# Score tiles of ten query rows by one transfer each, and a ring of eight tiles begun five steps ahead

## The chip, the cores and the metric

The kernel runs on one core of one Trainium2 chip. The metric is the device time of one execution in microseconds (us). A second value stands beside it in the profile: the span, from the first to the last instruction of the profiled execution.

## The reference

Attention whose heads are mixed before and after the softmax, then two MLP-mixer blocks. Only the attention is touched by the change:

```python
# q, k, v: (2, 12, 448, 64); w_pre, w_post: (12, 12)
scores = scale * np.matmul(q, k.transpose(0, 1, 3, 2))
scores = np.einsum('bhij,hg->bgij', scores, w_pre)
scores = scores - np.max(scores, axis=-1, keepdims=True)
attn = np.exp(scores)
attn = attn / (np.sum(attn, axis=-1, keepdims=True) + 1e-09)
attn = np.einsum('bhij,hg->bgij', attn, w_post)
return np.matmul(attn, v).astype(np.float32)
```

Behind it stand a token-mixing and a channel-mixing MLP (`_moe_ref`) and a gated MLP (`_moe2_ref`). They take about the last 320 us of the span.

## The kernel before

**Chunks.** Each of the two batches is cut into four chunks of 120, 120, 120 and 88 query rows. For a chunk, `qk` multiplies q by k for all twelve heads (six head pairs, six calls) and copies the result into a score tile S in SBUF: one query row to a partition, its 12 x 448 scores behind each other. S has two halves, partitions 0 to 63 and 64 to 127, and half of the chunk's rows stand in each. There are two buffers for S, so chunk x+2 overwrites chunk x.

**Steps.** The head mix contracts over heads, so heads must lie in partitions. `b_dma` therefore copies rows of S into tiles P with (query row, head) in the partitions: five query rows give 60 partitions. A step handles 20 query rows: two tiles P (r = 0, 1), each with two transfers of five rows (h = 0, 1) that land in partitions 0 to 59 and 64 to 123. A transfer's five source rows lie `nb` partitions apart: 12 in a chunk of 120, 8 in the chunk of 88. There are 23 steps to a batch, 46 in all; the last step of each chunk of 88 is half a step.

**What a step does.** `b_pre` (TensorE) multiplies the tiles P by a block-diagonal `wp`; `b_exp` takes the row maximum (VectorE) and the exponential (ScalarE); `b_norm` scales the post-mix weights (VectorE, GpSimd); `b_post` mixes heads after the softmax and turns the result (TensorE); `b_turn` copies it out of PSUM (VectorE). When a chunk's steps are done, `av` multiplies by v (TensorE), and VectorE and ScalarE copy its result.

**Order.** The order is written out by hand. Iteration i of the main loop issues `b_pre(i + LP)`, then `qk` for a later chunk, `b_exp(i + LP)`, `b_norm(i + 1)`, `b_post(i)`, `b_turn(i)`, `av` where a new chunk starts, and `b_dma(i + LD)`, with LD = 4 and LP = 2. So the transfers of a step stand two iterations ahead of the `b_pre` that reads them. The tiles P come from a pool of `NP_BUFS` = 2 (LD - LP + 1) = 6. The six `qk` calls of a chunk are spread over the iterations up to LD ahead of its first step, leaving out the iterations that have an `av`.

**Queues.** Every transfer of this stage but two is issued by SyncE (SP), in program order: the P transfers and the loads of q, k, v and, at the end of the stage, of weights. Each DMA also waits until the one issued eight before it has landed (eight semaphores in turn).

Of the kernel before, what the change touches and what calls it, by code (L numbers as in the profile page):

```python
# [8 lines left out]
F32 = mybir.dt.float32  # L9
# [7 lines left out]
AX = mybir.AxisListType  # L17
PSUM = bass.MemoryType.PSUM

LD, LP = 4, 2  # L20
NP_BUFS = 2 * (LD - LP + 1)

WB, RB, SQ = 3, 3, 5
# [7 lines left out]
def tile_kernel(ctx, tc, q, k, v, w_pre, w_post, w_tok1, w_tok2, w_ch1, w_ch2,  # L31
                w_u, w_v, g_ln, w_sg, b_sg, w_out, out):
    nc = tc.nc
    B, D, H, S = 2, 64, 12, 448
    P = 128
# [10 lines left out]
    IB = 10  # L46
    CH = [(0, 120), (120, 120), (240, 120), (360, 88)]
# [8 lines left out]
    xT = xpool.tile([P, NCC, T], F32, name="xT")  # L56
# [3 lines left out]
    wp = const.tile([P, 64], F32, name="wp")  # L60
# [167 lines left out]
    for n, w in enumerate(chw):  # L228
        p_ch.append(piece(w, P, NCC, P))
        if n in V_EARLY:  # L230
            j = V_EARLY[n]
# [3 lines left out]
    for o in GATE_ORDER.split():  # L235
        j = int(o[1])
# [40 lines left out]
    ap_ = actx.enter_context(tc.tile_pool(name="attn", bufs=1))  # L277
# [11 lines left out]
    vn, qn, KX, SS = {}, {}, {}, {}  # L289
# [32 lines left out]
    steps = []  # L322
# [8 lines left out]
    st = [dict() for _ in range(NB)]  # L331
    HB = IB // 2
    HW = HB * H
    NK = S // 64

    def b_dma(i):

        b, c, p, ne = steps[i]
        nb = CH[c][1] // IB
        ss = SS[b, c].rearrange("(a p) f -> a p f", a=2)  # L340
        st[i]["P"] = []
        for r in range(2):
            t = ap_.tile([P, S], F32, tag="P", name=f"P{i}_{r}", bufs=NP_BUFS)
            if ne == 2:
                j = 2 * p + r
                for h in range(2):
                    nc.sync.dma_start(out=t[64 * h:64 * h + HW],
                                      in_=SS[b, c][64 * h + j:64 * h + j + (HB - 1) * nb + 1:nb])
            else:
                m = CH[c][1] % (2 * IB) // 2  # L350
                r0 = 64 * r + HB * nb
                nc.sync.dma_start(out=t[:m * H], in_=SS[b, c][r0:r0 + m])
            st[i]["P"].append(t)

    def b_pre(i):
        b, c, p, ne = steps[i]
        rows = HW if ne == 2 else CH[c][1] % (2 * IB) // 2 * H
        ps = st[i]["pre"] = pair(psB, "B", f"pre{i}")
        for r, cols in enumerate(HALVES):
            for e in range(ne):  # L360
                rs = slice(64 * e, 64 * e + rows)
                nc.tensor.matmul(ps[cols, e, :S], lhsT=wp[rs], rhs=st[i]["P"][r][rs], start=True, stop=True)  # L362
        st[i]["P"] = None

    def b_exp(i):
        ne = steps[i][3]
# [10 lines left out]
    def b_norm(i):  # L377
# [6 lines left out]
        for e in range(ne):  # L384
            wt = ap_.tile([P, 64], F32, tag="wt", name=f"wt{i}_{e}", bufs=6)
            nc.gpsimd.tensor_scalar(wt[:, :HW], wd["post"], rr[:, e:e + 1], 1.0, op0=ALU.mult, op1=ALU.mult)  # L386
            st[i]["w"].append(wt)
# [4 lines left out]
    def b_post(i):  # L392
# [5 lines left out]
        for e in range(ne):  # L398
            E, wt = st[i]["e"][e], st[i]["w"][e]
            for s in range((NK + 1) // 2):  # L400
                for x, cols in enumerate(HALVES):
                    t = min(2 * s + x, NK - 1)
                    w = slice(0, HW) if 2 * s + 1 < NK else slice(x * HW // 2, (x + 1) * HW // 2)
                    o = e * 256 + s * HW
                    for r in range(2):
                        rs = slice(64 * r, 64 * r + HW)
                        nc.tensor.matmul(ps[cols, r, o:o + w.stop - w.start], lhsT=E[rs, t * 64:(t + 1) * 64],  # L407
# [10 lines left out]
    def av(b, c):  # L418
        s0, n = CH[c]
        nb = n // IB  # L420
        rest = n - nb * IB
        cols = IB * (nb + (rest > 0))
        ps = pair(psA, "A", f"av{b}_{c}")
        at = AT[b, c]
        for hp in range(NP):
            x, o = hp % 2, hp // 2 * cols
            for s in range(NK // 2):
                for j, out_rows in enumerate(HALVES):
                    w = vn[b, hp // 2][:, ((x * 2 + j) * (NK // 2) + s) * D:][:, :D]
                    nc.tensor.matmul(ps[out_rows, x, o:o + cols], lhsT=w,  # L430
                                     rhs=at[:, s * H + x * (H // 2) + hp // 2 * 2 + j, :cols],
                                     start=(s == 0 and hp < 2), stop=False, skip_group_check=True)
        for hp in range(NP):
            x, o = hp % 2, hp // 2 * cols
            for j, out_rows in enumerate(HALVES):
                nc.tensor.matmul(ps[out_rows, x, o:o + cols], lhsT=vn[b, hp // 2][HALVES[x], (12 + j) * D:(13 + j) * D],
                                 rhs=at[HALVES[x], NK // 2 * H + hp // 2 * 2 + j, :cols],
                                 start=False, stop=True, skip_group_check=True)
        s0 += b * S
        for x, copy in enumerate((nc.vector.tensor_copy, nc.scalar.copy)):  # L440
            src = ps[:, x, :NP // 2 * cols].rearrange("p (c k) -> p c k", k=cols)
            copy(xT[:, x::2, s0:s0 + nb * IB].rearrange("p c (i j) -> p c j i", j=nb),  # L442
                 src[:, :, :nb * IB].rearrange("p c (j i) -> p c j i", i=IB))
            if rest:
                h = rest // 2
                copy(xT[:, x::2, s0 + nb * IB:s0 + n].rearrange("p c (r i) -> p c r i", i=h),
                     src[:, :, nb * IB:].rearrange("p c (r i) -> p c r i", i=HB)[:, :, :, :h])

    CW = C // 2
# [35 lines left out]
    def turn_over(n):  # L485
        for _ in range(n):
            nc.tensor.matmul(idle[:, 0, :P], lhsT=ident, rhs=ident, start=True, stop=True)

    turn_over(8)
    scale_pre()  # L490
    both = ((psA, "A"), (psB, "B"), (psB, "B"))
    copies = (nc.scalar.copy, nc.vector.tensor_copy)
    for x in range(2):
        for i in range(NP):
            n = x * NP + i
# [29 lines left out]
    for i in range(-LD, NB):  # L525
# [35 lines left out]
        if i + LP >= NB:  # L561
            for _ in range(2):
                ps = pair(psB, "B", f"xps0_{len(turns)}")
# [95 lines left out]
    with ExitStack() as rctx:  # L659
# [5 lines left out]
        for f in range(NF):  # L665
            need(p_c1[f])
            w = parts(p_c1[f])
            for b in range(B):
                finish(*[U[cc, b] for cc in range(NCC)])
                ps = bank(f"c1ps{b}_{f}")  # L670
# [6 lines left out]
        for cc in range(NCC):  # L677
            pss = [bank(f"c2ps{b}_{cc}") for b in range(B)]
            for hf, pi in enumerate(p_c2[cc]):
                need(pi)  # L680
                w = parts(pi)
# [154 lines left out]
    for cc, b in [(0, 0), (1, 0), (0, 1), (1, 1)] + [(cc, b) for cc in range(2, NCC) for b in range(B)]:  # L836
# [3 lines left out]
        ps = bank(f"ops{b}_{cc}")  # L840
# [11 lines left out]
def layouts(q, k, v, w_pre, w_post, moe_w_tok1, moe_w_tok2, moe_w_ch1, moe_w_ch2,  # L852
            moe2_w_in, moe2_g_ln, moe2_w_sg, moe2_b_sg, moe2_w_out):

    import numpy as np

    def bits(a):

        return a.view(np.uint64) if a.dtype == np.float64 else a

    def rows(a, p):

        return bits(a).reshape(-1, p, a.shape[1]).transpose(1, 0, 2)

    def cols(a, p):

        return bits(a).reshape(a.shape[0] // p, p, -1, p).transpose(1, 2, 0, 3)

    def diagonal(w):
        h = w.shape[0]  # L870
        t = np.zeros((2, 64, 5, h), w.dtype)
        for i in range(5):
            t[:, i * h:(i + 1) * h, i] = w
        return t

    def halves(a):

        n = a.shape[-1] // 2
        nb = a.shape[-1] // 10
        rest = n - 5 * nb  # L880
        t = np.zeros((*a.shape[:-1], 2, 64), a.dtype)
        for h in range(2):
            t[..., h, :5 * nb] = a[..., h * 5 * nb:(h + 1) * 5 * nb]
            t[..., h, 5 * nb:n] = a[..., 10 * nb + h * rest:10 * nb + (h + 1) * rest]
        return t

    def tokens(w):

        t = np.concatenate([w.T, w.T])
        return t.reshape(-1, 128, t.shape[1]).transpose(1, 0, 2)  # L890

    B, H, S, D = q.shape
    qt = q.reshape(B, H // 2, 2, S, D).transpose(0, 2, 4, 1, 3).reshape(B, 2 * D, H // 2, S)
    qt = np.stack([halves(qt[..., s:s + 120]) for s in range(0, S, 120)], 2)
    whole = S // 128 * 128
    vs = v.reshape(B, H // 4, 2, 2, S, D)
    vt = vs[..., :whole, :].reshape(B, H // 4, 4, S // 128, 128, D).transpose(0, 4, 1, 2, 3, 5)
    vr = vs[..., whole:, :].transpose(0, 2, 4, 1, 3, 5).reshape(B, 128, H // 4, 2 * D)
    vt = np.concatenate([vt.reshape(B, 128, H // 4, -1), vr], -1)
    wp = diagonal(w_pre).reshape(128, 60)  # L900
    wq = diagonal(w_post).reshape(2, 64, 5, H // 4, 2, 2).transpose(0, 1, 4, 3, 5, 2).reshape(128, 60)
    half = moe2_w_in.shape[1] // 2
    arrays = {
        'q': qt,
        'k': k.reshape(B, H // 2, 2, S, D).transpose(0, 2, 4, 1, 3).reshape(B, 2 * D, H // 2, S),
        'v': vt,
        'w_pre': np.concatenate([wp, np.zeros((128, 4), wp.dtype)], 1),
        'w_post': wq,
        'w_tok1': rows(moe_w_tok1, S // 4),
        'w_tok2': rows(moe_w_tok2, 128),  # L910
        'w_ch1': cols(moe_w_ch1, 128),
        'w_ch2': cols(moe_w_ch2, 128),
        'w_u': cols(np.ascontiguousarray(moe2_w_in[:, :half]), 128),
        'w_v': rows(np.ascontiguousarray(moe2_w_in[:, half:]), 128),
        'g_ln': moe2_g_ln.reshape(-1, 128).T,
        'w_sg': tokens(moe2_w_sg),
        'b_sg': moe2_b_sg.reshape(1, S),
        'w_out': cols(moe2_w_out, 128),
    }
    return {n: np.ascontiguousarray(a) for n, a in arrays.items()}  # L920
# [34 lines left out]
```

## Time and profile before

| | us |
|---|---|
| median of 3 runs (lowest, highest) | 588.27 (586.41, 589.18) |
| the profiled execution | 587.66 |
| its span | 585.9 |
| the attention stage, in the span | about 13 to 266 |
| TensorE busy over the span | 549.0 |
| SyncE: issue of a P transfer, median | 0.737 |
| mean granted TensorE clock | 0.959 |

The profiled execution's time is 1.8 us above its span and 0.6 us below the median of the runs. TensorE (PE) is busy for 94% of the span, but a matmul that sits in the pipe counts as busy, so the chain of waits says more than the busy share. Lines of kernel.py are written L362 and so on; PEld is TensorE's weight load, SPq and the like are the engines' issue queues.

### The profile page before, as it was taken

The page shows a single profiled execution, that of the slowest core. Times are in us where ns is not written, and L with a number is a line of the kernel's source. Part 1 is how long each engine was busy: PE and PEld are TensorE (multiplying, and loading weights), DVE is VectorE, ACT ScalarE, POOL GpSimd, SP SyncE. Part 2 cuts the span into 40 slices and gives each one's busy share as a digit, 9 for nine tenths or more (in the row PEclk, how much of TensorE's full clock was granted, in tenths as well). Part 3 has the DMA queues.
Part 4 walks back from the last instruction along what each step waited for, and adds up shares of the span by engine and source line. Part 5 has one row for each costly group of instructions (what it writes and reads, how often), then busy time and mean ns, then how long its engine had stood idle before and what let it go on. Part 6 is the DMA issues. An engine that isn't in the chain of part 4 may idle for free.

```text
span 585.9 us, 14093 instructions
## 1 busy us (share of the span) xinstructions
PE 549.0 (94%) x5998; PEld 425.2 (73%) x5998; DVE 353.1 (60%) x537; ACT 239.3 (41%) x453; POOL 154.4 (26%) x185
## 2 busy tenths in 40 slices
PE   7999998889899989579999999999999999999997
PEld 4344655555455545358999999999999999888986
DVE  3354555344546543635835576777888786588882
ACT  3243545343535444634533334343333335455320
POOL 0010111011111111200492223234454454246600
PEclk9799999799989979759999999999999999999999
DMA  4365342323631315410312243434253332300332
GB/s 152 138 190 179 120 137 76 112 65 132 187 128 72 126 61 163 149 54 1 115 48 66 89 152 106 146 110 143 92 160 111 94 136 64 119 17 10 118 112 94
DMA packets 25647, 63.63 MB, mean 109 GB/s; under 512 B 2832, under 2 KB 18704, under 8 KB 25584
## 3 DMA queue, kind: packets, MB, share of 16 engines
q1 hardware_dynamic: 25296, 62.33, 32.8%
q8 instruction: 47, 0.77, 0.6%
q10 hardware_dynamic: 288, 0.39, 0.2%
q14 instruction: 16, 0.13, 0.1%
HBM read 40.70 MB, written 2.75 MB: 74 GB/s over the span
## 4 chain that ended last, share of the span: by engine, by line
PE 77%; DMA 13%; DVE 3%; ACT 3%; issue 2%; SPq 1%; POOLq 0%; POOL 0%; DVEq 0%; ACTq 0%
DMA P<-S 11%; PE pre L362 9%; PE av L430 5%; PE post L407 5%; PE c1ps L581 5%; PE c2ps L580 5%; PE c2ps L581 5%; PE c1ps L579 5%; PE c1ps L580 5%; PE c2ps L579 5%; PE qk L317 3%; PE ups L579 2%; PE ups L580 2%; PE ups L581 2%; PE vps L580 2%
## 5 line engine op out<-in xcount | busy, mean ns | idle before, releaser
L362 PE MATMUL pre<-P,wp 60*64 60x448 f32 x360 | 107.8, 587 | 12.2 <-DMA P<-S 11.4
L369 DVE TENSOR_REDUCE nm<-pre 128x2 f32<-128x896 f32 (+1 forms) x46 | 49.0, 1066 | 70.9 <-PE pre L362 70.7
L386 POOL TENSOR_SCALAR wt<-wd_post,rr 128x60 f32<-128x60 f32 x90 | 28.4, 329 | 215.5 <-DVE rr L382 174.0
L147 POOL TENSOR_TENSOR wl<-cv,wh 128x768 fp32r<-128x768 f32 x28 | 52.5, 1876 | 119.8 <-ACT wh L146 85.6
L407 PEld LDWEIGHTS post<-wt,E 60*64 60x64 f32 x2880 | 65.3, 145 | 23.0 <-issue 16.9
L374 ACT ACTIVATE E<-pre,nm 128x448 f32<-128x448 f32 x90 | 56.4, 634 | 44.4 <-DVE rc L380 34.7
L362 PEld LDWEIGHTS pre<-P,wp 60*64 60x64 f32 x360 | 24.9, 139 | 64.5 <-DMA P<-S 55.4
L407 PE MATMUL post<-wt,E 60*64 60x60 f32 (+1 forms) x2880 | 66.3, 230 | 3.8 <-ACT AT L415 2.9
L317 PE MATMUL qk<-kn,qn 64*64 64x448 f32 x384 | 58.6, 567 | 8.3 <-ACT xT L442 4.8
L319 ACT COPY S<-qk 128x896 f32<-128x896 f32 x42 | 38.1, 906 | 63.0 <-PE qk L317 59.6
L124 DVE SCALAR_TENSOR_TENSOR cv<-raw,cv 128x768 uint32<-128x768 uint32 (+3 forms) x44 | 53.2, 1209 | 1.3
L581 PE MATMUL c2ps<-r1h,wl 128*128 128x448 f32 x144 | 52.6, 365 | 0.0
L581 PE MATMUL c1ps<-uh,wl 128*128 128x448 f32 x144 | 52.6, 365 | 0.0
L580 PE MATMUL c2ps<-r1l,wh 128*128 128x448 f32 x144 | 52.6, 365 | 0.0
L579 PE MATMUL c1ps<-uh,wh 128*128 128x448 f32 x144 | 52.6, 365 | 0.0
L580 PE MATMUL c1ps<-ul,wh 128*128 128x448 f32 x144 | 52.6, 365 | 0.0
L579 PE MATMUL c2ps<-r1h,wh 128*128 128x448 f32 x144 | 52.6, 365 | 0.0
L415 DVE COPY AT<-post 128x840 f32<-128x840 f32 (+1 forms) x38 | 39.9, 1050 | 14.6 <-PE post L407 14.2
L102 ACT ACTIVATE cv<-raw 128x768 f32<-128x768 f32 (+3 forms) x44 | 36.1, 821 | 23.8 <-POOL wl L147 16.7
L126 DVE SCALAR_TENSOR_TENSOR cv<-raw,cv 128x768 uint32<-128x768 uint32 (+3 forms) x44 | 40.2, 914 | 1.1
L317 PEld LDWEIGHTS qk<-kn,qn 64*64 64x64 f32 x384 | 16.4, 135 | 30.2 <-issue 10.7
L120 DVE TENSOR_SCALAR cv<-cv 128x768 f32<-128x768 f32 (+3 forms) x44 | 30.2, 686 | 10.3 <-ACT cv L102 10.1
(187 smaller groups left out, 993.2 us busy)
## 6 DMA issues: line engine op xcount, KB each, us to landing
P<-S SPq DMA_DIRECT2D x176, 105.0 KB
raw<-in_w_ch_dram SPq DMA_DIRECT2D x24, 768.0 KB
raw<-in_w_v_dram SPq DMA_DIRECT2D x6, 512.0 KB
raw<-in_w_u_dram SPq DMA_DIRECT2D x4, 768.0 KB
raw<-in_w_out_dram SPq DMA_DIRECT2D x6, 512.0 KB
qn<-in_q_dram SPq DMA_DIRECT2D x14, 192.0 KB
vn<-in_v_dram SPq DMA_DIRECT2D x6, 448.0 KB
out_dram<-xT SPq DMA_DIRECT2D x12, 224.0 KB
```

The lines of the kernel that those rows point to most:

```text
L124: nc.vector.scalar_tensor_tensor(fi, lo, 29, fi, op0=ALU.logical_shift_right, op1=ALU.bitwise_or)
L126: nc.vector.scalar_tensor_tensor(fi, hi, 0xC0000000, fi, op0=ALU.bitwise_and, op1=ALU.bitwise_or)
L147: nc.gpsimd.tensor_tensor(dst[1], f, f32(dst[0]), op=ALU.subtract)
L317: nc.tensor.matmul(ps[cols, j, :S], lhsT=qn[b, c, i // QG][rows, i % QG, h], rhs=KX[b, i][rows], start=True, stop=True)
L362: nc.tensor.matmul(ps[cols, e, :S], lhsT=wp[rs], rhs=st[i]["P"][r][rs], start=True, stop=True)
L369: nc.vector.tensor_reduce(out=nm[:, :ne], in_=ps[:, :ne, :S], axis=AX.X, op=ALU.max, negate=True)
L374: nc.scalar.activation(t, ps[:, e, :S], AF.Exp, bias=nm[:, e:e + 1], scale=1.0, accum_out=sm[:, e:e + 1])
L407: nc.tensor.matmul(ps[cols, r, o:o + w.stop - w.start], lhsT=E[rs, t * 64:(t + 1) * 64], rhs=wt[rs, w], start=True, stop=True)
L415: copy(dst.rearrange("p g (a i) -> p a g i", i=HB), src.rearrange("p a (g i) -> p a g i", i=HB))
L579: nc.tensor.matmul(ps, lhsT=lh, rhs=rh, start=(start and i == 0), stop=False)
L580: nc.tensor.matmul(ps, lhsT=lh, rhs=rl, start=False, stop=False)
L581: nc.tensor.matmul(ps, lhsT=ll, rhs=rh, start=False, stop=(stop and i == n - 1))
```

## The change

`b_dma` makes one transfer for each tile: ten source rows, `nb` partitions apart, into partitions 4 to 123. Now `nb` is the number of steps of the chunk, so the ten rows lie 6 partitions apart in a chunk of 120 and 4 in the chunk of 88; they all lie in one half of S (tile r reads half r). A step has two transfers of 120 partitions where it had four of 60. The half step reads five rows where it read four. The tiles are eight fixed buffers `ring`, whose partitions 0 to 3 are set to zero once; `b_pre` reads partitions 0 to 63 and 64 to 123. LD is 5, so a step's transfers stand three iterations ahead of their `b_pre`, and the `qk` calls end one iteration earlier. The layouts of q, `w_pre` and `w_post` that the host prepares follow the new order of rows.

```diff
-LD, LP = 4, 2
+LD, LP = 5, 2
 NP_BUFS = 2 * (LD - LP + 1)
...
+    PAD = 64 - HW
     NK = S // 64
 
+    ring = [ap_.tile([P, S], F32, name=f"P{n}") for n in range(NP_BUFS)]
+
     def b_dma(i):
 
         b, c, p, ne = steps[i]
-        nb = CH[c][1] // IB
-        ss = SS[b, c].rearrange("(a p) f -> a p f", a=2)
-        st[i]["P"] = []
+        nb = CH[c][1] // (2 * IB)
         for r in range(2):
-            t = ap_.tile([P, S], F32, tag="P", name=f"P{i}_{r}", bufs=NP_BUFS)
-            if ne == 2:
-                j = 2 * p + r
-                for h in range(2):
-                    nc.sync.dma_start(out=t[64 * h:64 * h + HW],
-                                      in_=SS[b, c][64 * h + j:64 * h + j + (HB - 1) * nb + 1:nb])
-            else:
-                m = CH[c][1] % (2 * IB) // 2
-                r0 = 64 * r + HB * nb
-                nc.sync.dma_start(out=t[:m * H], in_=SS[b, c][r0:r0 + m])
-            st[i]["P"].append(t)
+            j = 64 * r + p
+            src = SS[b, c][j:j + (IB - 1) * nb + 1:nb] if ne == 2 else SS[b, c][64 * r + IB * nb:64 * r + IB * nb + HB]
+            nc.sync.dma_start(out=ring[(2 * i + r) % NP_BUFS][PAD:PAD + ne * HW], in_=src)
 
     def b_pre(i):
...
-                rs = slice(64 * e, 64 * e + rows)
-                nc.tensor.matmul(ps[cols, e, :S], lhsT=wp[rs], rhs=st[i]["P"][r][rs], start=True, stop=True)
-        st[i]["P"] = None
+                rs = slice(64 * e, 64 * e + 64 - PAD * e)
+                nc.tensor.matmul(ps[cols, e, :S], lhsT=wp[rs], rhs=ring[(2 * i + r) % NP_BUFS][rs], start=True, stop=True)
...
+    for t in ring:
+        nc.gpsimd.memset(t[:PAD], 0.0)
     turn_over(8)
```

SyncE's queue at the end of batch 0's chunk 2 and the start of its chunk 3. P16 and P17 below are the tiles of chunk 2's last steps, S0_3 is the score tile of chunk 3, qn1 the q of batch 1. Before:

```order
L347 DMA P16_0_1226<-S0_2_451 60x1x448 x2
L347 DMA P16_1_1229<-S0_2_451 60x1x448 x2
L347 DMA P17_0_1292<-S0_2_451 60x1x448 x2
L347 DMA P17_1_1295<-S0_2_451 60x1x448 x2
L347 DMA P18_0_1358<-S0_3_912 60x1x448 x2
L347 DMA P18_1_1361<-S0_3_912 60x1x448 x2
L299 DMA qn1_1_0_1364<-in_q_dram 128x384
```

The same place now (tiles are named by their place in the ring):

```order
L346 DMA P0_94<-S0_2_383 120x1x448
L346 DMA P1_95<-S0_2_383 120x1x448
L73 DMA gl_70<-in_g_ln_dram 128x4
L346 DMA P2_96<-S0_2_383 120x1x448
L346 DMA P3_97<-S0_2_383 120x1x448
L346 DMA P4_98<-S0_3_822 120x1x448
L346 DMA P5_99<-S0_3_822 120x1x448
L299 DMA qn1_1_0_1250<-in_q_dram 128x384
```

Two issues stand where four stood, and the load of q behind them stays where it was.

TensorE's queue from the `av` of chunk 0 on, up to the first `pre` of step 10 (qk0_2_4 and qk0_2_5 are the last two `qk` calls of chunk 2). Before:

```order
L436 MATMUL av0_0_714<-AT0_0_277,vn0_2_442 64x120 x4
L362 MATMUL pre9_773<-P9_0_651,wp_69 64x448 x2
L362 MATMUL pre9_773<-P9_1_654,wp_69 64x448 x2
L317 MATMUL qk0_2_4_778<-kn0_2_102,qn0_2_1_255 64x448 x4
L407 MATMUL post7_799<-wt7_0_675,E7_0_605 64x60 x12
L407 MATMUL post7_799<-wt7_0_675,E7_0_605 64x30 x4
L407 MATMUL post7_799<-wt7_1_677,E7_1_607 64x60 x12
L407 MATMUL post7_799<-wt7_1_677,E7_1_607 64x30 x4
L362 MATMUL pre10_839<-P10_0_765,wp_69 64x448 x2
L362 MATMUL pre10_839<-P10_1_768,wp_69 64x448 x2
L317 MATMUL qk0_2_5_844<-kn0_3_104,qn0_2_1_255 64x448 x4
```

The same place now:

```order
L427 MATMUL av0_0_698<-AT0_0_279,vn0_2_447 64x120 x4
L354 MATMUL pre9_753<-P2_96,wp_69 64x448 x2
L354 MATMUL pre9_753<-P3_97,wp_69 64x448 x2
L317 MATMUL qk0_2_5_758<-kn0_3_112,qn0_2_1_257 64x448 x4
L398 MATMUL post7_779<-wt7_0_659,E7_0_593 64x60 x12
L398 MATMUL post7_779<-wt7_0_659,E7_0_593 64x30 x4
L398 MATMUL post7_779<-wt7_1_661,E7_1_595 64x60 x12
L398 MATMUL post7_779<-wt7_1_661,E7_1_595 64x30 x4
L354 MATMUL pre10_817<-P4_98,wp_69 64x448 x2
L354 MATMUL pre10_817<-P5_99,wp_69 64x448 x2
L317 MATMUL qk0_3_0_823<-kn0_0_102,qn0_3_0_376 64x448 x4
```

The last `qk` of chunk 2 now stands right behind the `av`, one iteration earlier than before, and the next chunk's first `qk` has taken its old place; the number of matmuls is the same.

## Rows read from the trace of the kernel before

**Rows 1.** The page: chain shares by line; two groups (busy, mean ns); P transfers

```profile
DMA P<-S 11%; PE pre L362 9%; PE av L430 5%; PE post L407 5%; PE c1ps L581 5%; PE c2ps L580 5%; PE c2ps L581 5%; PE c1ps L579 5%; PE c1ps L580 5%; PE c2ps L579 5%; PE qk L317 3%; PE ups L579 2%; PE ups L580 2%; PE ups L581 2%; PE vps L580 2%
...
L369 DVE TENSOR_REDUCE nm<-pre 128x2 f32<-128x896 f32 (+1 forms) x46 | 49.0, 1066 | 70.9 <-PE pre L362 70.7
...
L415 DVE COPY AT<-post 128x840 f32<-128x840 f32 (+1 forms) x38 | 39.9, 1050 | 14.6 <-PE post L407 14.2
...
P<-S SPq DMA_DIRECT2D x176, 105.0 KB
```

**Rows 2.** Windows between ends of av: length, engines' busy time (count), clock, DMA share, GB/s

```profile
15.00:62.90 47.90, 45.26 (x668) 22.29 (x664) 21.07 (x34) 16.37 (x42) 4.78 (x16) 0.93 0.53 168
62.90:90.70 27.80, 26.23 (x580) 15.54 (x576) 14.95 (x26) 13.65 (x31) 4.01 (x14) 1.00 0.36 123
90.70:122.10 31.40, 28.38 (x588) 17.02 (x584) 14.82 (x25) 14.45 (x32) 3.61 (x12) 0.89 0.27 86
122.10:145.80 23.70, 21.90 (x464) 12.50 (x460) 11.50 (x21) 11.00 (x24) 2.70 (x9) 1.00 0.31 106
145.80:176.40 30.60, 27.61 (x580) 16.05 (x576) 14.76 (x26) 13.48 (x32) 3.59 (x12) 0.94 0.48 157
176.40:202.80 26.40, 25.20 (x581) 15.18 (x576) 14.84 (x26) 13.65 (x31) 3.59 (x12) 1.00 0.26 96
202.80:233.70 30.90, 26.76 (x548) 15.76 (x544) 12.12 (x24) 14.49 (x32) 3.58 (x12) 0.89 0.36 113
233.70:265.60 31.90, 20.93 (x356) 16.07 (x348) 15.23 (x32) 13.48 (x26) 4.07 (x6) 0.63 0.31 95
```

**Rows 3.** The chain of waits from 92 us: start, length, what

```profile
92.39 0.98 PE qk L317 x8
93.37 0.90 PE post L407 x64
94.28 0.78 PE pre L362 x8
95.06 0.75 PE qk L317 x8
...
99.24 5.37 DMA P<-S
```

**Rows 4.** The chain of waits at an av, from 117 us

```profile
117.44 3.84 PE av L430 x72
121.28 0.82 PE av L436 x24
...
122.12 0.80 DVE xT L442
...
122.94 0.79 ACT xT L442
```

**Rows 5.** The chain of waits in the first steps

```profile
15.75 3.25 DMA P<-S
...
46.02 7.78 DMA P<-S
```

**Rows 6.** SyncE's issues by line: ns, shortest/median/longest; first and last start

```profile
L347 SPq DMA_DIRECT2D P<-S x176: 720/737/1729, 13.2 to 227.2; - x176
L352 SPq DMA_DIRECT2D P<-S x4: 647/666/1340, 116.1 to 230.9; - x4
...
L299 SPq DMA_DIRECT2D qn<-in_q_dram x14: 334/488/1246, 2.8 to 159.5; - x14
```

**Rows 7.** Timeline of SyncE: start, length, issues

```profile
13.20 9.46 SPq L347 DMA_DIRECT2D P<-S  x12
```

**Rows 8.** Windows in which P transfers run back to back (columns as in Rows 2)

```profile
84.50:92.50 8.00, 7.04 (x174) 5.81 (x170) 4.01 (x6) 2.12 (x5) 0.60 (x2) 1.00 0.34 124
...
211.00:213.00 2.00, 0.58 (x16) 0.27 (x9) 0.17 (x1) 2.00 (x5) 0.60 (x2) 1.00 0.30 97
215.00:219.00 4.00, 4.00 (x58) 2.37 (x61) 0.87 (x1) 0.00 (x0) 0.00 (x0) 0.50 0.27 88
```

More of the change, by code (lines that the diff above doesn't have):

```diff
@@ L333, in tile_kernel @@
     HW = HB * H
+    PAD = 64 - HW
     NK = S // 64
+    ring = [ap_.tile([P, S], F32, name=f"P{n}") for n in range(NP_BUFS)]
     def b_dma(i):
         b, c, p, ne = steps[i]
-        nb = CH[c][1] // IB
-        ss = SS[b, c].rearrange("(a p) f -> a p f", a=2)
-        st[i]["P"] = []
+        nb = CH[c][1] // (2 * IB)
         for r in range(2):
-            t = ap_.tile([P, S], F32, tag="P", name=f"P{i}_{r}", bufs=NP_BUFS)
-            if ne == 2:
-                j = 2 * p + r
-                for h in range(2):
-                    nc.sync.dma_start(out=t[64 * h:64 * h + HW],
-                                      in_=SS[b, c][64 * h + j:64 * h + j + (HB - 1) * nb + 1:nb])
-            else:
-                m = CH[c][1] % (2 * IB) // 2
-                r0 = 64 * r + HB * nb
-                nc.sync.dma_start(out=t[:m * H], in_=SS[b, c][r0:r0 + m])
-            st[i]["P"].append(t)
+            j = 64 * r + p
+            src = SS[b, c][j:j + (IB - 1) * nb + 1:nb] if ne == 2 else SS[b, c][64 * r + IB * nb:64 * r + IB * nb + HB]
+            nc.sync.dma_start(out=ring[(2 * i + r) % NP_BUFS][PAD:PAD + ne * HW], in_=src)
     def b_pre(i):
-        b, c, p, ne = steps[i]
-        rows = HW if ne == 2 else CH[c][1] % (2 * IB) // 2 * H
+        ne = steps[i][3]
         ps = st[i]["pre"] = pair(psB, "B", f"pre{i}")
@@ L445, in av @@
                 h = rest // 2
-                copy(xT[:, x::2, s0 + nb * IB:s0 + n].rearrange("p c (r i) -> p c r i", i=h),
+                copy(xT[:, x::2, s0 + nb * IB:s0 + n].rearrange("p c (i r) -> p c r i", r=2),
                      src[:, :, nb * IB:].rearrange("p c (r i) -> p c r i", i=HB)[:, :, :, :h])
@@ L870, in diagonal @@
         h = w.shape[0]
-        t = np.zeros((2, 64, 5, h), w.dtype)
+        t = np.zeros((2, 64, h, 5), w.dtype)
         for i in range(5):
-            t[:, i * h:(i + 1) * h, i] = w
+            t[:, h * i:h * (i + 1), :, i] = w
         return t
     def halves(a):
-        n = a.shape[-1] // 2
-        nb = a.shape[-1] // 10
-        rest = n - 5 * nb
         t = np.zeros((*a.shape[:-1], 2, 64), a.dtype)
         for h in range(2):
-            t[..., h, :5 * nb] = a[..., h * 5 * nb:(h + 1) * 5 * nb]
-            t[..., h, 5 * nb:n] = a[..., 10 * nb + h * rest:10 * nb + (h + 1) * rest]
+            t[..., h, :a.shape[-1] // 2] = a[..., h::2]
         return t
@@ L899, in layouts @@
     vt = np.concatenate([vt.reshape(B, 128, H // 4, -1), vr], -1)
-    wp = diagonal(w_pre).reshape(128, 60)
-    wq = diagonal(w_post).reshape(2, 64, 5, H // 4, 2, 2).transpose(0, 1, 4, 3, 5, 2).reshape(128, 60)
+    wp = diagonal(w_pre).transpose(0, 1, 3, 2).reshape(2, 64, 60)
+    wp = np.pad(wp, ((0, 0), (0, 0), (0, 4)))
+    wp[0] = np.roll(wp[0], 4, 0)
+    wq = diagonal(w_post).reshape(2, 64, H // 4, 2, 2, 5).transpose(0, 1, 3, 2, 4, 5).reshape(128, 60)
     half = moe2_w_in.shape[1] // 2
@@ L906, in layouts @@
         'v': vt,
-        'w_pre': np.concatenate([wp, np.zeros((128, 4), wp.dtype)], 1),
+        'w_pre': wp.reshape(128, 64),
         'w_post': wq,
```

## The prediction

> **What bounds the kernel now.** I read the chain of waits by line first, then the windows between two `av`, then the chain piece by piece where it passes through a transfer, then the issues on SyncE and the windows in which only P transfers run. The chain spends 11% of the span, 64 us, in `DMA P<-S`, more than in any matmul [rows 1]. All of it lies in the attention stage, which the ends of the `av` cut into eight periods [rows 2]. A period with six steps takes 26.4 to 31.4 us.
>
> How long would such a period be if no tile were late? Where none is, the chain shows a step of TensorE alone: `qk` 0.98 or 0.75 us, `post` 0.90, `pre` 0.78 [rows 3], so 0.75 + 0.90 + 0.78 = 2.43. VectorE needs about the same for a step, 1.07 for the maximum and 1.05 for the turn [rows 1] beside some 0.3 of small work. Then a 5.37 us transfer ends the run [rows 3]. An `av` takes 3.84 + 0.82 = 4.66, and the next `qk` waits for two copies of 0.80 and 0.79, of which one `pre` hides 0.78: about 0.9 lost [rows 4]. Six steps with six `qk` and one `av` make 6 x (0.78 + 0.90) + 0.98 + 5 x 0.75 + 4.66 + 0.9 = 20.4 us. The periods are 6 to 11 us longer than that.
>
> Why are tiles late? A step needs four P transfers of 105 KB (107.5 thousand bytes). Back to back they move 124 GB/s at a DMA share of 0.34, that is 0.34 x 16, about five engines [rows 8]: 0.87 us a transfer, 3.47 a step, against the 2.43 that TensorE wants. SyncE is hardly faster: twelve issues take 9.46 us, 0.79 each [rows 7]. As the queue fills, landing takes 7.78 us instead of 3.25 [rows 5]. So five DMA engines set the pace, with SyncE close behind.
>
> A window in the chunk of 88 rows looks different: 97 and 88 GB/s, at shares of 0.30 and 0.27 [rows 8]. There the five source rows stand 8 partitions apart instead of 12, so the distance of the rows costs something: 107.5/97 to 107.5/88, 1.11 to 1.22 us a transfer instead of 0.87.
>
> **The change part by part.**
>
> *Engines to a tile.* Five source rows keep five engines busy [rows 8]. I take one engine to a source row, so ten for a tile now, each still moving one row's twelve pieces. If nothing else changed, a tile of twice the bytes would land in the same 0.87 us. The Trainium skill ("DMA: Bandwidth & Descriptors", section on why a DMA increments its semaphore by 16) says that the largest number up to 16 that divides the outer sizes of both sides is taken: 5 for 5 rows and 60 partitions, 10 for 10 rows and 120. By that rule, the trace's share agrees for 5; no run here shows 10.
>
> *Distance of the rows.* This speaks against the change. Rows 6 or 4 apart, ten in one half, are closer than the 8 that already cost bandwidth. The lower bound of a tile is 0.87 (no loss), the upper bound that a pair of rows goes at the rate of one engine: one engine moves 124/5 = 24.8 GB/s, two rows are 43 thousand bytes, so 1.73 us. The rows with a distance of 8 gave 1.11 to 1.22 for what is, per engine, the same work, and I take 1.2, which they are nearest to. The Trainium skill ("SBUF — State Buffer", section on the DMA port swizzle) gives the reason: groups of four partitions share ports, and partitions 32 apart share one. By it, rows 8 apart have one such pair (0 and 32), rows 12 apart none, and ten rows at a distance of 6 two or three pairs; the trace agrees on the first two. If a port carried just one engine's rate all the time, a tile would cost the upper bound.
>
> *Issue.* A transfer of 60 partitions takes SyncE 0.72 us, one of 48 0.65 [rows 6]; on that line 120 take 0.72 + 60 x (0.073/12) = 1.09. Bounds: 0.33 (the quickest load of 128 partitions, rows 6) and 2 x 0.737 = 1.47. I take 1.09, with 0.05 between issues 1.14, so two to a step are 2.3 instead of 3.1. Transfer and issue overlap; the slower, 1.2, sets the pace: 2.4 us a step, equal to TensorE's 2.43 and below a period's mean of 20.4/6 = 3.4.
>
> *LD and the ring.* A chunk's first tiles can't be read before its last `qk` is copied. Before, two iterations lie between: post 0.90, then pre, qk, post, qk 3.18, so 4.1 us, against a copy of 0.9, four issues of 0.78 and 2.5 to land (3.25 less its own issue, rows 5), 6.5: 2.4 late in each chunk. Now a third iteration adds 2.43: 6.5 us, against 0.9 + 2 x 1.14 + 2.5 = 5.7. The wait fits with 0.8 to spare, though the last `qk` now stands behind the `av`. Behind such a transfer SyncE holds the loads of q or v, which are wanted a chunk later. I leave one late tile, 1.2 us, in every period.
>
> *The rest.* Eight memsets on GpSimd run while q and k load; TensorE's `pre` has the same columns, so costs the same; the half step moves five rows for four, on a tile that no longer waits. Conversion of weights begins one iteration earlier, on VectorE and ScalarE, which are busy for about half of a period [rows 2]. I cost these at nothing; were the first memsets not covered, they would delay the first `pre` by under 1 us.
>
> *The sum.* From the first issue at 13.2 [rows 7] to the first `av`'s end, nine steps of tiles are needed: 18 x 1.2 = 21.6, the seven loads of q, v and k that SyncE issues among them at about 0.55 (0.488 and the gap, rows 6) 3.9, landing 2.5, then pre, qk, post and `av` 7.1. That ends at 48.3, not 62.9: 14.6 us saved. Here SyncE and transfers still pace. The six-step periods become 20.4 + 1.2 = 21.6: of 27.8, 31.4, 30.6 and 26.4, 6.2 + 9.8 + 9.0 + 4.8 = 29.8 saved. The period of 23.7 has a half step, so one and a half steps less, 21.6 - 1.5 x 1.68 = 19.1: 4.6. The one of 30.9 holds weight conversions and steps without `qk`, where VectorE and ScalarE set the pace; the other six-step periods lose 26% (29.8 of 116.2), and I take somewhat less, 21%: 6.5. The last, 31.9, is mostly transposes at half clock (0.63 granted, rows 2); 2 of it is waits on transfers. Together 14.6 + 29.8 + 4.6 + 6.5 + 2 = 57.5. The profiled execution took 587.66, so 530; the median shown is 0.6 higher. The 320 us behind the stage stay as they are.
>
> **The rivals.**
>
> *Ten rows never run faster than a pair allows, or the tile still gets five engines.* Either way a tile takes 1.73 us and a step 3.47, as now. For it: rows 8 apart lost bandwidth with one pair in five, and now there are more. Against: that loss was 22 to 29%, not half. The port section of the Trainium skill named above, read strictly, is this rival. Then the first period ends at 13.2 + 31.1 + 3.9 + 2.5 + 7.1 = 57.8 (5.1 saved), and a six-step period needs 12 x 1.73 + loads about 1.5 + a late tile 1.7 = 24.0 (3.8, 7.4, 6.6, 2.4), the short one 21.2 (2.5), the seventh 5, the last 2: 34.8 saved, 553.
>
> *A wait at the chunk's start replaces the one removed.* Landing may take as long as it did in the chain, 5.37 instead of 3.25 [rows 3, 5], or issue costs 1.47. Then the 0.8 to spare becomes 1.3 late; with what that shifts, some 1.7 in each of seven chunks: 12 back, 542. For it: the last `qk` is behind the `av`. Against: the queue is empty when SyncE waits there.
>
> *Slower.* The ten engines together carry no more than the close rows did, 88 GB/s. A tile of 215 thousand bytes takes 2.44 us, a step 4.9. The P stream ran from 13.2 to 231 [rows 6], 218 us for 46 steps; less 26 loads (12 of q, 6 of v, 4 of k, 4 of weights) at 0.55, 4.4 a step. It would be 46 x 0.5 = 23 longer: 611. It decides below 215/2.2 = 98 GB/s. Against: two of the five rows lost, and the other three kept going.
>
> **How the numbers follow.** Forecast 62% (its own range 519 to 540), 553 for the pair or five engines 17%, 542 for the wait 14%, slower 5%, no change 2%. The likeliest gives 530. Its lower end is a tile at the issue's 1.14 with no late tile: 8 periods x 1.2 and 18 x 0.06, about 11 less. Towards the slow side the range must reach past 553 to leave two in ten out: 516 to 557. About 0.5% is what a measurement of this kernel tells from no change. Faster by more 93%, within it 2%, slower 5%.
>
> **What would show it.** In the profile after: 92 transfers; an issue near 1.09 us; a DMA share near 10/16 and over 170 GB/s where tiles run back to back; `DMA P<-S` in the chain down from 11% to 2 or 3%; six-step periods of 21 to 22 us; the granted clock at 1.0 through the stage. It is wrong if the share stays at 0.34, if back-to-back tiles move under 130 GB/s, or if the chain still enters a transfer at each chunk's start.

## The result and the profile after

The changed kernel takes 545.02 us (median of four runs, 542.0 to 551.58), the kernel before 587.34: a ratio of 0.9266, interval 0.9204 to 0.9328. Disturbed runs, that of 551.58 here and two of the four of the kernel at 547.33 further down among them, are left out of all ratios. The profiled execution took 544.84 with a span of 543.1, so 42.8 us of span are gone; the prediction's sum had 57.5. The time lies inside the range given (516 to 557), 15 us above the forecast of 530.

The page of the changed kernel, the chain's shares by engine and by line and the row of P transfers, answers to [rows 1]:

```profile
PE 79%; ACT 7%; DVE 6%; DMA 6%; issue 2%; SPq 0%; POOLq 0%; POOL 0%; ACTq 0%; DVEq 0%
PE post L398 6%; PE av L421 6%; PE c2ps L574 5%; PE c1ps L574 5%; PE c1ps L572 5%; PE c2ps L572 5%; PE c1ps L573 5%; PE c2ps L573 5%; PE qk L317 5%; DMA P<-S 3%; PE pre L354 3%; ACT E L365 2%; PE ups L573 2%; PE ups L572 2%; PE ups L574 2%
...
P<-S SPq DMA_DIRECT2D x88, 210.0 KB
```

`DMA P<-S` went from 11% of the span to 3%. The 88 transfers have 210 KB each; with the four of the half steps they are the 92 forecast. What came up in the chain are ScalarE and VectorE. The same line before:

```profile
PE 77%; DMA 13%; DVE 3%; ACT 3%; issue 2%; SPq 1%; POOLq 0%; POOL 0%; DVEq 0%; ACTq 0%
```

SyncE's issues of P transfers (shortest, median, longest, in ns), which answer to [rows 6]:

```profile
L346 SPq DMA_DIRECT2D P<-S x92: 768/811/1968, 13.3 to 181.3; - x92
```

The windows of the changed kernel: its eight periods, the end of one `av` to the next, as in [rows 2], then two stretches in which tiles run almost alone, as in [rows 8], and one in which tiles and loads run together:

```profile
13.30:52.90 39.60, 34.19 (x696) 18.92 (x696) 22.10 (x35) 18.47 (x44) 4.82 (x16) 0.96 0.75 211
52.90:76.30 23.40, 21.36 (x580) 14.82 (x576) 14.82 (x26) 13.67 (x31) 4.05 (x14) 1.00 0.50 150
76.30:99.90 23.60, 21.29 (x588) 13.72 (x584) 14.80 (x25) 14.47 (x32) 3.61 (x12) 1.00 0.42 128
99.90:117.80 17.90, 16.16 (x464) 10.39 (x460) 11.38 (x21) 10.90 (x24) 2.72 (x9) 1.00 0.44 134
117.80:143.20 25.40, 22.06 (x580) 14.38 (x576) 14.65 (x26) 13.49 (x32) 3.61 (x12) 1.00 0.58 175
143.20:165.40 22.20, 20.31 (x581) 13.53 (x576) 14.68 (x25) 13.67 (x31) 3.61 (x12) 1.00 0.38 120
165.40:192.90 27.50, 19.58 (x540) 14.32 (x536) 12.70 (x26) 15.67 (x34) 3.90 (x12) 0.88 0.48 140
192.90:223.30 30.40, 18.41 (x356) 14.39 (x348) 17.27 (x32) 13.12 (x25) 4.85 (x7) 0.61 0.26 80
...
148.00:160.00 12.00, 11.08 (x352) 6.63 (x351) 9.87 (x17) 9.52 (x23) 2.41 (x8) 1.00 0.59 187
16.00:22.00 6.00, 4.19 (x24) 0.90 (x16) 2.38 (x3) 2.10 (x5) 0.00 (x0) 1.00 0.59 181
...
28.00:46.00 18.00, 15.05 (x332) 8.00 (x328) 10.25 (x17) 10.44 (x25) 2.87 (x10) 0.91 0.88 234
```

From 148 to 160 us the share is 0.59, 9.4 of 16 engines, where five rows had 0.34 [rows 8]. At 187 GB/s a tile of 215 thousand bytes costs 215/187 = 1.15 us, at the 181 of the first steps 1.19; 1.2 was predicted.

Period by period, in us of span:

| period | before | after | saved | predicted |
|---|---|---|---|---|
| first, nine steps of tiles | 62.9 (its end) | 52.9 (its end) | 10.0 | 14.6 |
| 2, six steps | 27.8 | 23.4 | 4.4 | 6.2 |
| 3, six steps | 31.4 | 23.6 | 7.8 | 9.8 |
| 4, short | 23.7 | 17.9 | 5.8 | 4.6 |
| 5, six steps | 30.6 | 25.4 | 5.2 | 9.0 |
| 6, six steps | 26.4 | 22.2 | 4.2 | 4.8 |
| 7 | 30.9 | 27.5 | 3.4 | 6.5 |
| 8 | 31.9 | 30.4 | 1.5 | 2 |

The rest, 320 us, is as long as before. The granted clock is 1.00 from the second period to the sixth, where two of these had 0.89 and 0.94 [rows 2]. The missing 15 us lie in the first period (4.6), the third and second (2.0 and 1.8), the fifth (3.8) and the seventh (3.1); the fourth gained 1.2 more than forecast. The third is the clearest, since its chain holds no transfer at all. The changed kernel's chain of waits in it (start, length, what):

```profile
79.87 0.78 PE pre L354 x8
80.65 0.80 PE qk L317 x8
...
81.47 0.55 ACT S L319
82.02 0.25 issue
82.27 1.35 ACT E L365 x4
83.62 0.81 ACT S L319
...
84.47 0.98 PE qk L317 x8
85.45 0.91 PE post L398 x64
...
91.94 0.95 PE post L398 x64
92.91 1.08 DVE AT L406
94.12 1.13 PE post L398 x56
95.26 3.84 PE av L421 x72
```

The tiles are in time here, and the period still takes 23.6 us, not 21.6. Between two `qk` the chain leaves TensorE for ScalarE: a copy of scores, the exponentials, another copy. That happens twice in the period. At its end, the last `post` ahead of the `av` waits for VectorE's turn.

### The profile page after: what moved, and what is told of

Same layout as the page of the kernel before. It is cut to its first block, busy times and chain, and to the rows that moved or that the text cites. A ratio compares the mean times of both kernels' runs of the same rounds, so it can differ in the third digit from the quotient of the medians.

```text
span 543.1 us, 14017 instructions
## 1 busy us (share of the span) xinstructions
PE 498.2 (92%) x5998; PEld 408.4 (75%) x5998; DVE 353.4 (65%) x536; ACT 240.8 (44%) x454; POOL 157.7 (29%) x193
## 4 chain that ended last, share of the span: by engine, by line
PE 79%; ACT 7%; DVE 6%; DMA 6%; issue 2%; SPq 0%; POOLq 0%; POOL 0%; ACTq 0%; DVEq 0%
PE post L398 6%; PE av L421 6%; PE c2ps L574 5%; PE c1ps L574 5%; PE c1ps L572 5%; PE c2ps L572 5%; PE c1ps L573 5%; PE c2ps L573 5%; PE qk L317 5%; DMA P<-S 3%; PE pre L354 3%; ACT E L365 2%; PE ups L573 2%; PE ups L572 2%; PE ups L574 2%
## 5 line engine op out<-in xcount | busy, mean ns | idle before, releaser
L398 PEld LDWEIGHTS post<-wt,E 60*64 60x64 f32 x2880 | 54.9, 141 | 37.3 <-issue 26.8
L398 PE MATMUL post<-wt,E 60*64 60x60 f32 (+1 forms) x2880 | 55.8, 224 | 13.8 <-ACT AT L406 9.7
L317 PE MATMUL qk<-kn,qn 64*64 64x448 f32 x384 | 48.3, 563 | 11.9 <-ACT xT L433 4.8
L354 PE MATMUL pre<-P,wp 64*64 64x448 f32 (+1 forms) x360 | 53.5, 557 | 5.6 <-DMA P<-S 4.1
L102 ACT ACTIVATE cv<-raw 128x768 f32<-128x768 f32 (+3 forms) x44 | 36.2, 824 | 23.5 <-POOL wl L147 16.7
L317 PEld LDWEIGHTS qk<-kn,qn 64*64 64x64 f32 x384 | 13.8, 135 | 35.7 <-ACT S L319 14.1
L146 ACT CAST wh<-cv 128x768 fp32r<-128x768 f32 x28 | 23.4, 836 | 32.7 <-DVE cv L126 32.0
```

Of the source, the lines that this page charges most:

```text
L317: nc.tensor.matmul(ps[cols, j, :S], lhsT=qn[b, c, i // QG][rows, i % QG, h], rhs=KX[b, i][rows], start=True, stop=True)
L354: nc.tensor.matmul(ps[cols, e, :S], lhsT=wp[rs], rhs=ring[(2 * i + r) % NP_BUFS][rs], start=True, stop=True)
```

## The experiments

**The two halves of the change, each alone.** First the transfers with the old lead:

```diff
-LD, LP = 5, 2
+LD, LP = 4, 2
```

> The changed kernel with LD back at 4, so a ring of six tiles begun four steps ahead; the transfers of ten rows stay. Theory (the gain comes from ten engines working on a tile instead of five): most of the gain stays, 548 to 556 us; the first tiles of a chunk come late again, by 1 to 2 us in each of seven chunks, and back-to-back tiles move about 187 GB/s as in the changed kernel. Rival (the gain comes from starting five steps ahead): 575 us or more, since the lead is that of before.

Then the kernel before with only the new lead (and so a pool of eight tiles):

```diff
-LD, LP = 4, 2
+LD, LP = 5, 2
```

> The kernel before with LD = 5 alone: four transfers of five rows a step, a pool of eight tiles begun five steps ahead. Theory (ten engines): 574 to 586 us, because the five engines at 124 GB/s still need 3.47 us for a step's tiles and only the waits at the start of a chunk (about 2 us in each of up to seven) shrink. Rival (the lead): 555 us or less.

Measured: 552.37 us, ratio 0.9385 (0.9318 to 0.9452), and 573.83, ratio 0.9778 (0.9709 to 0.9848); the kernel before took 588.22. So the lead alone is worth 14 us, the transfers alone 36, both 43: most of the gain is the transfers, and the lead adds some 7 to them. The new transfers double the engines and halve the issues at once, and no run separates the two. By [rows 7] four issues a step keep SyncE busy for 4 x 9.46/12 = 3.15 us, so by estimate ten engines with four issues could have brought a step's tiles from 3.47 us to 3.15 at best. The halved issues alone are not enough either: adjacent rows, below, have them too, and lose. What the lead removes shows in the chain of the first of these kernels (new transfers, old lead):

```profile
62.27 5.50 DMA P<-S
...
85.96 4.10 DMA P<-S
...
107.62 4.59 DMA P<-S
```

Once in each chunk the chain enters a transfer, as it does before the change [rows 3]. With a lead of five these steps are gone from batch 0 after the first period. The periods shrink by less than 4 to 5 us, from 25.4, 24.1 and 20.6 (the second to the fourth) to 23.4, 23.6 and 17.9, because other waits come out from under them.

**The distance of the rows.** One kernel reads ten rows 13 apart across both halves of S, one ten adjacent rows; the transfers are as many and as large, but tiles then hold other rows than the step's.

```diff
-            j = 64 * r + p
-            src = SS[b, c][j:j + (IB - 1) * nb + 1:nb] ...
+            j = p + 5 * r
+            src = SS[b, c][j:j + (IB - 1) * 13 + 1:13] ...
```

> The changed kernel with the ten source rows of a tile 13 partitions apart, five from each half of S; it reads other rows than the reference does, the same number and size of transfers. By the port rule no two of the ten rows share a port. Theory (row distance costs bandwidth): back-to-back tiles go from about 187 to 220 to 245 GB/s, the landing under load is shorter, and the time falls to 535 to 542 us, most of it in the first period where loads and tiles compete. Rival (the distance of the rows costs nothing; 187 GB/s is what SyncE's issue allows): 545 us within 2, and the same 187 GB/s.

```diff
-            src = SS[b, c][j:j + (IB - 1) * nb + 1:nb] ...
+            src = SS[b, c][j:j + IB] ...
```

> The changed kernel with the ten source rows of a tile next to each other; it reads other rows than the reference does, the same number and size of transfers. By the port rule up to four rows share a port. Theory (row distance costs bandwidth): a tile takes 2.5 to 3.5 us instead of 1.15, tiles set the pace through the whole stage, and the time rises to 610 to 700 us. Rival (the distance costs nothing): 545 us within 2.

Measured: rows 13 apart 542.38 us, ratio 0.9234 (0.9164 to 0.9303); adjacent rows 603.31, ratio 1.0234 (1.0151 to 1.0317), slower than the kernel before, though less than the 610 expected. The page's chain by line of the kernel with adjacent rows, and the first steps, where tiles run almost alone, with adjacent rows and with rows 13 apart:

```profile
DMA P<-S 17%; PE av L421 5%; PE c2ps L572 5%; PE c1ps L573 5%; PE c2ps L573 5%; PE c1ps L574 5%; PE c1ps L572 5%; PE c2ps L574 5%; PE post L398 4%; PE pre L354 3%; PE qk L317 3%; SPq L346 2%; PE ops L573 2%; PE ups L573 2%; PE ups L574 2%
```

```profile
16.00:22.00 6.00, 1.73 (x10) 0.54 (x8) 1.09 (x1) 0.53 (x1) 0.00 (x0) 0.83 0.54 92
16.00:22.00 6.00, 5.34 (x40) 1.46 (x32) 3.93 (x5) 2.75 (x5) 0.00 (x0) 1.00 0.65 237
```

With adjacent rows the share is nearly as high as in the changed kernel, 0.54 against 0.59, but 92 GB/s pass instead of 181: the engines are occupied and the bytes come slower, 2.3 us a tile (2.5 to 3.5 was expected). That is below the 98 from which the slower rival was to decide. That rival is real, then, with rows closer than the change has them. The Trainium skill ("SBUF — State Buffer", section on the DMA port swizzle) lets groups of four partitions share a port; ten adjacent rows crowd on three or four. By that, the trace agrees, with 92 GB/s.

Rows 13 apart get 237 GB/s, as expected (220 to 245): 0.91 us a tile where 6 apart take 1.19. So the distance of 6 costs about a quarter of the rate. It costs little time: the medians are 2.6 us apart and their intervals overlap. In the two profiles 5.2 us of span lie between the kernels, and about half of it in the first period, which ends at 50.4 us instead of 52.9; the fifth is 1.3 shorter. The third stays at 23.6: transfers no longer set that period.

**Waits on ScalarE, and the loads.** `qk` spread over every iteration, also those with an `av`, so that fewer share one iteration; then the loads of k and v for batch 1 moved to later iterations; then both.

```diff
-        room = [s for s in range(f0 + 1, f1 + 1) if s not in starts]
+        room = list(range(f0 + 1, f1 + 1))
```

> The changed kernel with a chunk's six qk calls spread over all iterations up to its first transfer, the one with the av too, so that no iteration of a six-step chunk has two. Theory (what the waits on tiles left behind is ScalarE: where an iteration has two qk, the second copy to S stands behind the two exponentials, and the next qk waits for its PSUM buffer; the chain shows that twice in the period from 76.3 to 99.9 us): 1.5 to 3 us less in most periods, 533 to 540 us. Rival (the copy only moves to another place and waits there, behind the av's copies): 545 us within 2.

```diff
-        add(4 + g, load_k, 1, g)
+        add(9 + g, load_k, 1, g)
...
-        add(first[1, 0] + 1 + g, load_v, 1, g)
+        add(first[1, 0] + 3 + g, load_v, 1, g)
```

> The changed kernel with the loads of k for batch 1 issued five iterations later and those of v for batch 1 two later. Theory (in the first period and in the one from 117.8 to 143.2 us the tiles wait behind loads on the same engines; a DMA share of 0.88 at 234 GB/s from 28 to 46 us): 3 to 5 us less in the first period and 2 to 5 in the other, 536 to 541 us. Rival (the loads cost the same wherever they stand): 545 us within 2, the waits turn up in the periods that the loads were moved to.

> Both at once, qk spread over all iterations and the loads of k and v for batch 1 later. If both theories hold and the two act in different places: the sum of their gains within 3 us, 526 to 534 us. If one of them only uncovers the other's wait: no better than the better of the two.

Measured: 541.42 (0.9223, 0.9178 to 0.9267), 543.39 (0.9254, 0.9187 to 0.9321) and 543.36 (0.9246, 0.92 to 0.9292). None is outside the changed kernel's interval, and all three miss the ranges of their theories. Spreading takes the third period to 23.0; moving the loads takes the first from 39.6 to 38.3 and the fifth from 25.4 to 24.1, while the second and the sixth grow by 0.9 each (24.3 and 23.0). The loads do lie in the way: in the changed kernel's chain a tile of the fifth period is waited for at 130.99 for 5.68 us, with v being loaded ahead of it. Moved, they come in the way elsewhere, or too late. In that kernel's chain a tile of the second period is waited for, and in the fifth the `av` waits for v itself:

```profile
62.29 6.71 DMA P<-S
...
132.47 7.09 DMA vn<-in_v_dram
```

**Rows 12 apart, with the right rows.** The host puts query nb i + t of a chunk (nb its number of tiles) into partition 12 i + t, so that a tile reads ten rows 12 apart over both halves. Three kernels build on it: `qk` spread as above; the second score copy of an iteration on VectorE; spread and loads moved.

```diff
-        nb = CH[c][1] // (2 * IB)
+        nb = CH[0][1] // IB
...
-            j = 64 * r + p
-            src = SS[b, c][j:j + (IB - 1) * nb + 1:nb] if ne == 2 else ...
+            j = 2 * p + r
+            src = SS[b, c][j:j + (ne * HB - 1) * nb + 1:nb]
```

> The changed kernel with the queries laid out so that a tile's ten rows lie 12 partitions apart over both halves of S (all rows of the reference are read). By the port rule no two of them share a port. Theory (close rows cost bandwidth, but only the places where tiles are late gain): as with rows 13 apart, 538 to 543 us, back-to-back tiles at 220 GB/s or more, the first period 2 to 3 us shorter, the periods of batch 0 that hold no late tile unchanged at 23.6 us. Rival (rows 13 apart looked a little faster by chance): 545 within 2.

> Rows 12 apart and the six qk calls spread over all iterations. Theory (both tiles and ScalarE's queue hold up the stage, and taking one away uncovers the other): together 6 to 12 us below the changed kernel, 533 to 539 us, the six-step periods with no pair of qk at 21 to 22 us. Rival (VectorE and the copies behind av set a floor near 23 us for a period): no better than either alone, 540 to 543 us.

```diff
             for d in due[1:]:
-                qk(*d)
+                qk(*d, copy=nc.vector.tensor_copy)
```

> Rows 12 apart, qk where the changed kernel has it, and the second copy to S of an iteration on VectorE instead of ScalarE. Theory (the second copy waits behind the exponentials in ScalarE's queue): the chain's pieces of exponential and copy to S go, 1 to 2 us less in each six-step period, 531 to 538 us. Rival (VectorE, with 2.4 us of its own in a step, has no room for a copy of 1.1 us): the wait moves to the turn and the row maximum, 540 to 546 us.

> Rows 12 apart, qk spread, and the loads of k and v for batch 1 later. Theory (loads and tiles compete on the same engines in the first period and in the first of batch 1): 2 to 4 us below rows 12 apart with qk spread. Rival (with tiles at full rate the loads no longer matter): the same within 2 us.

Measured: 539.17 us, ratio 0.9157 (0.9115 to 0.9199); 540.66 (0.918, 0.9135 to 0.9224); 547.33 over all its runs, ratio 0.9231 (0.917 to 0.9292); 540.63 (0.9205, 0.9159 to 0.925). The first has the lowest ratio of all: its interval lies below that of the changed kernel, though each comes from its own comparison with before, and the three that build on it overlap with the changed kernel. Its window of the first steps, against 181 GB/s in the changed kernel, and that of tiles and loads together, against 234:

```profile
16.00:22.00 6.00, 3.87 (x20) 0.89 (x16) 2.82 (x3) 1.77 (x5) 0.00 (x0) 1.00 0.65 235
...
28.00:46.00 18.00, 15.40 (x430) 10.30 (x424) 11.70 (x21) 10.78 (x26) 3.00 (x10) 1.00 0.86 257
```

Its first period ends at 48.7 us, 4.2 earlier than in the changed kernel and close to the 48.3 of the prediction. Its third is at 23.6 again. Spreading `qk` on top takes the third to 22.8 and the fourth from 17.9 to 16.7, but the first ends 2.0 later and the fifth grows from 23.9 to 25.1, so that nothing is gained in all. One thing that it costs shows in its chain (the end of the third period):

```profile
89.60 0.78 PE qk L317 x8
...
90.40 0.92 ACT S L319
...
91.36 4.22 PE av L421 x72
```

A `qk` in the iteration of the `av` makes the `av` wait for its copy, and the `av` itself takes 4.22 instead of 3.84. Copying on VectorE gains nothing either.

**The exponentials behind the copy.** By then two accounts of the 23.6 us were open: the second copy waits in ScalarE's queue behind the exponentials, or the scores pass through one buffer of PSUM (`psA`), so that a `qk` waits for the copy of the one before, whatever ScalarE does in between. The last kernel, on rows 12 apart, cuts the exponentials off `b_exp` and puts them behind the second copy; the maximum stays in place.

```diff
         nc.vector.tensor_reduce(out=nm[:, :ne], in_=ps[:, :ne, :S], axis=AX.X, op=ALU.max, negate=True)
         sm = ...
+
+    def b_act(i):
...
             for d in due[1:]:
                 qk(*d)
+        if 0 <= i + LP < NB:
+            b_act(i + LP)
+        if i >= 0:
             b_turn(i, nc.vector.tensor_copy if i <= LAST else nc.scalar.copy)
```

> The version with rows 12 apart over both halves, in which the exponentials of a step stand behind the second score copy of the iteration in ScalarE's queue; the row maximum stays where it was. Theory: a period of six steps takes 23.6 us and not 20.4 because the second copy waits in order behind the exponentials, and the next score matmul for that copy; in the chain 0.55 + 0.25 + 1.35 + 0.81 = 2.96 us stand for a post and a pre of 1.68, so 1.28 us are lost twice in a period. Then the exponentials leave the chain and the periods of six steps come to about 21 to 21.5 us; with some 2 us in each of six periods, 527 to 532 us. Rival: one score buffer in PSUM, the turn copies and the tiles hold a period at 22.8 us, as with the score matmuls spread over more iterations; then it comes to 535 to 540 us, or above where the late exponentials make post wait.

Measured: 541.26 us, ratio 0.9226 (0.9172 to 0.928), and the third period takes 23.5 where 21 to 21.5 was expected. The theory of the queue's order fell. The chain of this kernel at the same place:

```profile
74.97 0.80 PE qk L317 x8
...
75.78 0.92 ACT S L319
...
76.74 1.03 PE qk L317 x8
...
77.79 0.92 ACT S L319
...
78.75 0.98 PE qk L317 x8
```

The exponentials have left the chain, and from one `qk` to the `qk` after the pair it is still 78.75 - 74.97 = 3.78 us, against 84.47 - 80.65 = 3.82 in the changed kernel. `qk`, copy, `qk`, copy alternate, and the exponentials had only filled that time. That fits VectorE's copies, which brought nothing: another engine doesn't shorten the alternation. That the one buffer in PSUM causes it is read from the chain and not tested by itself.

## Why the prediction was right, and where its sum was off

**The number: partly luck.** The transfers did what was forecast of them, but 545 lies outside the forecast's own range, 519 to 540. What holds it is the range's upper part, drawn to take in the rival at 553. It is also 3 us from the rival of a wait at the chunk's start (542), whose wait isn't in the chain.

**The bound, engines and tile: right.** Five engines set the pace before; ten work now (0.59 of 16), a tile takes 1.15 us, and the chain's share of transfers fell to 3%. The Trainium skill ("DMA: Bandwidth & Descriptors", section on why a DMA increments its semaphore by 16) gives ten engines for 10 rows and 120 partitions. By that rule, the trace agrees at 9.4.

**Distance of the rows: right in size, with one place missed.** Where only tiles run, six apart take 1.15 to 1.19 us a tile, 12 and 13 apart 0.91, near the lower bound of 0.87; the 1.2 held. It rested on two windows, and the one at 88 GB/s also holds the start of a weight load (SyncE issues it at 217.94 us), so 97 is the cleaner of the two. From 28 to 46 us tiles compete with the loads of q, k and v: the share is 0.88, and 234 GB/s pass where rows 12 apart get 257. The prediction gave these loads SyncE's time to issue and no bandwidth. The changed kernel's chain waits for a tile there, and once more in the fifth period:

```profile
38.59 7.76 DMA P<-S
...
130.99 5.68 DMA P<-S
```

The kernel with rows 12 apart ends the first period 4.2 us earlier, of the 4.6 that were missing. One profile each stands behind this; in three others with rows 12 apart it ends at 47.1, 47.3 and 50.8 us.

**Issue: mis-sized, in the harmless direction.** The line through 48 and 60 partitions gave 1.09 us for 120; measured is 0.811. The transfer, not the issue, sets the pace as forecast (adjacent rows and rows 13 apart have the same number of issues and differ by 61 us), so nothing in the sum hangs on it.

**The lead: right.** After the first period no transfer stands in the chain of batch 0. The rival of a wait there is what the old lead does with the new transfers, 552 us.

**The step that failed: the base of 20.4 us for a period of six steps.** Periods of 21 to 22 us were to show it; they take 22.2 to 25.4. The base was a sum over TensorE with the one loss at the `av`, taken from a stretch where no tile was late and no two `qk` met [rows 3]. Three things are missing in it. The third period holds seven `qk`, not six, counted in the changed kernel's windows of `qk` alone (56 instructions, 8 to a `qk`; columns: PE, PEld, clock, DMA share, GB/s):

```profile
52.90:76.30 23.40, 6.42 (x48) 2.09 (x48) 1.00 0.50 150
76.30:99.90 23.60, 6.78 (x56) 1.66 (x56) 1.00 0.42 128
```

Two iterations of it have a pair of `qk`. A pair with its two copies takes 3.82 us (80.65 to 84.47) where the base has 2 x 0.75 + 0.90 + 0.78 = 3.18, and the `qk` behind it 0.98 instead of 0.75: 0.87 a pair. And in the iteration that ends in the `av`, which has no `qk`, `post` waits for VectorE's turn: 94.12 + 1.13 - 92.89 = 2.36 us (the wait and its `post`) stand for a `pre` and a `post`, 1.68. Together 20.4 + 0.75 + 2 x 0.87 + 0.68 = 23.6, as measured. With rows 6, 13 and 12 apart the period takes the same 23.6, so the transfers have no part in it. The base was thus 3.2 us too short here; 1.2 of that didn't show, because the sum also allowed one late tile, which didn't come. That late tiles covered these 3.2 before the change is inferred, not shown.

**The rest.** The fifth period has the 5.68 us behind the loads of v, where 1.2 was allowed for a late tile; that this makes its 3.8 is read from the chain, since moving the loads put another wait there. The seventh, at 27.5, was an estimate by shares; no run separates what fills it. The second period's chain holds no transfer: it has one pair (4.17 us, 57.43 to 61.60) and the wait for the turn ahead of the `av`; what makes the rest of its 1.8 stays open. The fourth came out at 17.9 instead of 19.1 by errors that partly cancel: the sum gave it no pair, but six `qk` where it has five, a late tile, and the `av` of a long chunk, 4.66, where that of 88 rows took 2.94 + 0.63 = 3.57. A second score buffer in PSUM, the direct test of the alternation, wasn't tried.

**The rivals.** Tiles at half rate, 553 us, didn't come: 1.15, not 1.73. Slower didn't either, but adjacent rows show that its price exists.

## What to carry to other kernels

When a late transfer is removed, the period becomes the longest of the chains that the transfer covered, so work out that floor from the worst iteration (two products through one PSUM buffer, the last `post` ahead of an `av`), not from the quietest stretch of the trace. Give a copy between partitions an outer size that puts more engines to work, and set its source rows well apart: the distance alone made 542 or 603 us of the same transfers. Before an engine's order is blamed for a wait in the chain, move that work away and see whether the length stays.

## What the runs showed of the hardware

An issue on SyncE hardly grows with the partitions, 0.737 us for 60 and 0.811 for 120 (medians), but it is longer where transfers are slow, up to 1.97 us in the changed kernel, and 1.43 in the median with adjacent rows:

```profile
L346 SPq DMA_DIRECT2D P<-S x92: 768/1428/3117, 13.0 to 239.0; - x92
```

The share of busy DMA engines doesn't tell the rate. In the first steps, 0.54 went with 92 GB/s for adjacent rows, 0.59 with 181 for rows 6 apart and 0.65 with 237 for rows 13 apart.
